# Attention into a mixture of experts on one core: every score tile in two PSUM banks of its own, one bank shared by the second attention product and the transposes of q, and a planner with other durations

## The chip, the core and the metric

The kernel runs on one core of a Trainium2 chip. The core has TensorE (PE, matrix products; its weight loads are listed as PEld), VectorE (DVE), ScalarE (ACT), GpSimd (POOL) and SyncE (SP, which here only issues DMAs). Matrix products are written to PSUM, eight banks of 2 KB in each of 128 partitions, so 512 float32 values wide; PE writes PSUM, DVE and ACT read it. The metric is the device time of one execution in microseconds, less is better. Before the change three runs took 2241.11, 2243.8 and 2248.19 us, median 2243.8.

## What is computed

```python
# attention: 4 batches of 12288 queries, 128 channels
kv_pool = kv.reshape(B, H // r, r, W // r, r, C).mean(axis=(2, 4))   # 768 keys for each batch
k = v = kv_pool.reshape(B, -1, C) @ w_sr
s = scale * (q @ k.T);  a = softmax(s);  x = a @ v                   # x: 49152 rows of 128
# mixture of experts on x: 8 experts, one for each row
logits = normalized(x) @ normalized(expert_emb).T / tau
e = argmax(logits);  gate = softmax(logits)[e]
out = gate * (relu(x @ w1[e]) @ w2[e])                               # w1: 128 x 1024, w2: 1024 x 128
```

## The kernel before

Every float32 operand of a large product is split into two float16 halves, hi and lo, and the product is made of three float16 products (hi x hi, hi x lo, lo x hi).

**Attention** runs in 96 steps of 512 queries. For each step, q is scaled, transposed and split (`q_mul`, `q_t`, `q_hi`, `q_lo`; the transposes by PE into the PSUM tile `pq`, from step 45 on by a DMA instead). Then for each of four groups of 128 queries: the score product of 128 x 768 (`s_mm`, L608, six matmuls), its negated maximum on DVE (`s_max`, L613), the scaled bias (`s_bias`, L625), the exponential on ACT (`s_exp`, L631), and the split of the result p into halves (`p_hi`, L649, and `p_lo`, L659). The halves are turned by DMA (`p_t`, L664). The second product (`av`, L679, eighteen matmuls of 137 columns for one group) writes two groups side by side into one bank, the tile `xp`; DVE inverts the sums (`x_norm`, L690 and L691), ACT or DVE scales the rows (`x_mul`, L699 or L701), and after some copies the rows are scattered to HBM by expert (`g_scatter`, POOL).

**Groups.** After every four steps a chain of small DVE and PE instructions finds each row's expert and place (`g_logits`, `g_count`, `g_rank`, `g_place`; counts in the PSUM tile `rk`), and another, on POOL and DVE in turn, chooses which tiles the experts work on (`select`, L1029 to L1081).

**Experts** take tiles of 512 rows (88 of them), then of 256 rows. A tile is loaded transposed (`load`), its expert's weights are fetched (`load_w`), and it runs in eight units: the first layer (`l1`, L1298, three matmuls of 512 columns into the tile `ph`), its two halves hh on ACT (`h_hi`, L1305) and hl on DVE (`h_lo`, L1310), and the second layer (`l2`, L1331, twelve matmuls into the tile `po`). The result is scaled (`o_out`, L1340) and scattered.

**PSUM.** In the first `ka` steps attention is alone: two score tiles of three banks, each with two scores of 768 columns side by side, so that the middle bank belongs to both (`s_tiles`, L330); and two single banks (`ps_1`, `ps_2`) in turn for everything else that goes through `one_tile`: xp, pq, rk, the products of the keys. From step `ka` on the pools are exchanged (`swap_banks`): one score tile of three banks, two banks for ph, one for po, one for xp, and one (`ps_1`) for all the rest. Instructions of two engines that touch one bank wait for each other. The step before that, `KX = KA - 1`, is the first whose xp comes from the new pool.

**The order.** The program is written in the order that a planner finds (class `Plan`). Every operation is put in by `add` with an engine, a duration in microseconds, a due time and what it waits for; the planner runs an event list over the engines, and an engine takes the ready operation that is due first. Due times come from the table `X`: lengths of a step (`da`, `di`, `db`, before, beside and after the experts) and offsets within it in eighths of a step (`av`, `l2`, `p`, `s`, `x`, `r`), or in microseconds. `turn(tag, n)` makes an operation wait for the users of the buffer n turns back, `take` and `free` hold a bank of `one_tile`. The planner lets a score wait for the score four turns back in the first stage and two turns back in the second, though the middle bank ties neighbours:

```python
tag, nb = ("s", 4) if k < KA else ("s1", 2)
o = add("PE", 0.98, key, lambda j=j: s_mm(k, j), hi, lo, *deps, *turn(tag, nb))
```

Of the kernel before, what the change touches and what calls it, by code (L numbers as in the profile page):

```python
# [33 lines left out]
P_LO = {"D": 0.87, "P": 1.6}  # L34
# [4 lines left out]
X = dict(  # L39
    ka=22, da=6.919, di=15.197, db=12.403, dma=1.46, ahead=3.016, av=9.0, av0=0.39, l2=1.971, qt=5.647,  # L40
    lead=15.443, x=4.072, r=2.598, s=-2.823, p=10.466, x0=18.227, r0=19.685, s0=2.117, p0=10.054, qt0=1.742,
    pm="cabcbcacccbccbccccacaa", pl="aaaaaaaa", nm="DD", xn="A", nm0="D", xn0="DA", we="dcdadcddaddcddcd",
    h=5.625, kv=6.596, kvs=0.535, w0=-23.865, start=21.505, early=28.723, wd=10.527, xw=0.77, qd=45, qs=4.44,
    ql=8.549, v0=47.946, m=1.536, end=-1.246, ne=-9.661, ge=-97.983,
)
# [3 lines left out]
def attention_moe(  # L49
# [280 lines left out]
    s_tiles = [ps_s.tile([P, 2 * NK], F32, name=f"s_{i}") for i in range(2)]  # L330
# [268 lines left out]
    def s_mm(k, j):  # L599
        n = NQ * k + j  # L600
        o = n % 2 * NK
        t = s_tiles[n // 2 % len(s_tiles)]
        qs, kk = ks[k]["qT"][:, j], st[k // SPB]["k"]
        cuts = (0, 256, NK) if o else (0, 512, NK)
        for lo, hi in zip(cuts, cuts[1:]):
            terms = ((0, kk[0]), (0, kk[1]), (1, kk[0]))
            for i, (l, r) in enumerate(terms):
                nc.tensor.matmul(t[:, o + lo : o + hi], qs[:, l, :], r[:, lo:hi], start=i == 0, stop=i == 2)  # L608
        ks[k]["s", j] = t[:, o : o + NK]
# [59 lines left out]
    def av(k, j):  # L669
        h, i = divmod(j, 2)  # L670
        if i == 0:
            name = f"xp{k}_{h}"
            t = one_tile(name) if k < KX else ps_h.tile([P, 512], F32, tag="xp", name=name, bufs=1)
            ks[k]["xp", h] = t[:, : 2 * VW].rearrange("p (j c) -> p j c", c=VW)
        (hi, lo), v = (ks[k]["pt", h, n][:, i] for n in range(2)), v2[k // SPB % 2]
        w = C + E + 1
        for c in range(NCH):
            for n, (l, r) in enumerate(((hi, v[0]), (hi, v[1]), (lo, v[0]))):
                nc.tensor.matmul(  # L679
                    ks[k]["xp", h][:, i, :w], l[:, c, :], r[:, c, :w], start=c == 0 and n == 0,  # L680
                    stop=c == NCH - 1 and n == 2,
                )
# [632 lines left out]
    def l2(t, u):  # L1315
        n = size(t)
        fu = 512 // n
        if u == 0:
            tag = "xp" if t >= NA and t % 2 else "po"
            ts[t]["po"] = ps_h.tile([P, n], F32, tag=tag, name=f"po{t}", bufs=1)  # L1320
# [31 lines left out]
    KX = KA - 1  # L1352
# [155 lines left out]
    def step_ops(k):  # L1508
# [3 lines left out]
        if k % 2 == 0:  # L1512
# [9 lines left out]
            qa = add("DVE", 0.65, key + 0.5, lambda: q_scale(k), *sqs, k_scale[b])  # L1522
# [19 lines left out]
        tag, nb = ("s", 4) if k < KA else ("s1", 2)  # L1542
        for j in range(NQ):
# [52 lines left out]
        for j in range(NQ):  # L1596
            h, i = divmod(j, 2)
            key = slot(k + 1, at(k, "av") + 2 * j)
            deps = [o] if j else [v_ready[b]]
            if i == 0 and k >= KX:  # L1600
                deps += [x_swap, *turn("xp", 1)]
# [4 lines left out]
            if i == 0 and k >= KX:  # L1606
                took("xp", o)
# [3 lines left out]
            if i:  # L1611
                v = add("DVE", 0.38, key + 1.2, lambda h=h: x_norm(k, h), o, *([n] if h else turn("x", 2)))
                eng = in_turn("xn", k, 2 * k + h)
                n = add(
                    eng, 0.42 if eng == "ACT" else 0.36, key + 1.5, lambda h=h: x_mul(k, h), v,
                    free=f"xp{k}_{h}" if k < KX else None,
# [4 lines left out]
                if k >= KX:  # L1621
                    reads("xp", v, n)
# [3 lines left out]
        lo = add("POOL", 1.2, key + at(k, "r"), lambda: x_lo(k), hi)  # L1626
# [5 lines left out]
    def group_ops(g, t):  # L1632
# [12 lines left out]
        for i, fn in enumerate(places):  # L1645
# [6 lines left out]
            add("POOL", 1.28, t + 1.28 * i, lambda i=i: g_scatter(g, i), pc[-1], gc[-1], dma=0.22) for i in range(GT)  # L1652
# [5 lines left out]
        if g >= 2:  # L1658
# [3 lines left out]
            for i, fn in enumerate(select(n, base[(n + 3) % 3])):  # L1662
                eng, dur = ("DVE", 0.15) if fn.__name__ in SELECT_DVE else ("POOL", 0.3)
# [40 lines left out]
    for t in range(NTILE):  # L1704
# [8 lines left out]
        lw = took("wb", add("POOL", 1.35, s - X["lead"] - 1.0, lambda t=t: load_w(t), *deps[:2], *stores, *turn("wb", WB), dma=2.92))  # L1713
        o1 = o2 = None
        f = 512 / size(t)
        for u in range(nu):
# [7 lines left out]
            po = "xp" if not whole and t % 2 else "po"  # L1724
            o2 = add("PE", 0.68, k2, lambda t=t, u=u: l2(t, u), hi, lo, o2, *(turn(po, 1) if u == 0 else ()))
# [9 lines left out]
            add("POOL", 1.28, k2 + 4.0 + 1.28 * j, lambda t=t, j=j: o_scatter(t, j), o, dma=0.2) for j in range(size(t) // P)  # L1735
# [42 lines left out]
```

## Time and profile before

| | |
|---|---|
| median of three runs | 2243.8 us (2241.11 to 2248.19) |
| the profiled execution | 2243.36 us, span 2241.7 us |
| PE busy | 1975.5 us, 88% of the span |
| DVE, ACT, POOL busy | 79%, 68%, 65% |
| score products | 53.8 to 1960.8 us |
| experts' products | 391.7 to 2230.0 us |

In the lines below, `out<-in` names the tiles without buffer numbers; "x" is a count, and a duration in a group is its mean. A line of the waits reads: engine and line that waited, engine and line that ended the wait, microseconds in total, times, the longest. In the timeline a row begins with its start and duration, and brackets give the idle time of the engine before it and what ended it. PEclk is the granted TensorE clock in tenths of full speed. The order shows what stands on an engine one after the other, with no times; line numbers there are those of the kernel it is taken from, and those of the changed kernel lie two to ten lower or higher than before.

### The profile page before, as it was taken

The numbers are of one execution on the slowest core, as the hardware profiler recorded it, in microseconds if no ns is written. First come the engines' busy times: TensorE is split into PE (matmuls) and PEld (weight loads), VectorE is DVE, ScalarE is ACT, GpSimd is POOL, SyncE is SP. The second block draws the span as 40 slices with busy tenths as digits, with TensorE's granted clock in tenths as the row PEclk, the third lists the DMA queues.
The fourth block names the chain that finished last, engine by engine and source line by source line (L and its number), as shares of the span: only waits on it lengthen the run. The fifth ranks groups of instructions, "written<-read, shape, count | busy, mean of one in ns | idle before, by whom it ended". The sixth has DMA issues, their size and how long they took to land.

```text
span 2241.7 us, 57429 instructions
## 1 busy us (share of the span) xinstructions
PE 1975.5 (88%) x21516; PEld 1492.5 (67%) x21516; DVE 1765.4 (79%) x3863; ACT 1531.3 (68%) x3158; POOL 1464.9 (65%) x1932
## 2 busy tenths in 40 slices
PE   5776765988999889898999998999999999999998
PEld 4455554766777666676766776666777766776697
DVE  6877788888878878888878878888888878865655
ACT  3677776687777667776767776777777777754443
POOL 1435268877677686686686686876686576677454
PEclk9788997999999999999999999999999999999999
DMA  8897799978778678997888897978887787743233
GB/s 233 188 209 157 156 181 197 183 149 140 158 131 151 136 137 166 167 180 137 141 158 156 137 169 143 207 146 154 134 155 145 133 160 120 134 79 81 50 86 79
DMA packets 896123, 331.86 MB, mean 148 GB/s; under 512 B 842706, under 2 KB 854107, under 8 KB 894048
## 3 DMA queue, kind: packets, MB, share of 16 engines
q1 hardware_dynamic: 853504, 258.60, 64.8%
q0 software_dynamic: 39968, 68.29, 11.0%
q8 instruction: 171, 2.80, 0.5%
q10 hardware_dynamic: 2368, 1.25, 0.2%
q14 instruction: 112, 0.92, 0.1%
HBM read 170.55 MB, written 64.50 MB: 105 GB/s over the span
## 4 chain that ended last, share of the span: by engine, by line
DVE 27%; PE 27%; POOL 17%; ACT 13%; issue 12%; DMA 4%; POOLq 0%; SPq 0%; DVEq 0%; ACTq 0%
POOL xs_rows L183 8%; PE po L1331 7%; PE s L608 7%; PE ph L1298 7%; DVE plo L659 7%; DVE nm L613 6%; ACT p L631 6%; PE xp L679 5%; DVE hl L1310 5%; POOL out_dram L183 3%; ACT phi L649 2%; ACT hh L1305 2%; POOL t_part L1023 2%; ACT x L699 1%; DVE nm L625 1%
## 5 line engine op out<-in xcount | busy, mean ns | idle before, releaser
L1305 ACT ACTIVATE hh<-ph 128x512 f16<-128x512 f32 x776 | 463.2, 597 | 340.4 <-PE ph L1298 286.0
L1310 DVE SCALAR_TENSOR_TENSOR hl<-ph,hh 128x512 f16<-128x512 f32 x776 | 530.0, 685 | 141.1 <-ACT hh L1305 135.9
L1298 PE MATMUL ph<-x,wbuf 128*128 128x512 f16 (+1 forms) x2544 | 623.5, 362 | 1.8 <-DVE hl L1310 1.3
L1331 PE MATMUL po<-wbuf,hh 128*128 128x128 f16 x6208 | 610.9, 219 | 8.3 <-DVE o L1340 8.2
L1331 PE MATMUL po<-wbuf,hl 128*128 128x128 f16 x3104 | 560.2, 220 | 36.1 <-DVE hl L1310 34.4
L608 PE MATMUL s<-k,qT 128*128 128x512 f16 (+1 forms) x2304 | 454.0, 336 | 134.4 <-ACT p L631 98.4
L1331 PEld LDWEIGHTS <-hh 128*128 128x128 f16 x6208 | 498.5, 98 | 80.1 <-issue 13.2
L631 ACT ACTIVATE p<-s,nm,qa 128x768 f32<-128x768 f32 x384 | 380.2, 991 | 249.1 <-DVE nm L625 136.6
L183 POOL DMA_INDIRECT out_dram<-o,m x388 | 415.7, 1071 | 183.5 <-issue 101.0
L183 POOL DMA_INDIRECT xs_rows<-rows,pi x384 | 421.6, 1098 | 120.0 <-issue 101.6
L679 PE MATMUL xp<-v,pthi 128*128 128x137 f16 x4608 | 467.5, 227 | 24.1 <-DVE x L701 18.0
L659 DVE TENSOR_TENSOR plo<-p,phi 128x768 f16<-128x768 f32 x371 | 402.8, 1087 | 69.3 <-ACT phi L649 64.2
L679 PEld LDWEIGHTS <-pthi 128*128 128x128 f16 x4608 | 385.2, 100 | 100.5 <-issue 32.5
L608 PEld LDWEIGHTS <-qT 128*128 128x128 f16 x2304 | 228.2, 100 | 326.8 <-issue 177.8
L679 PE MATMUL xp<-v,ptlo 128*128 128x137 f16 x2304 | 444.4, 226 | 0.6 <-DMA ptlo<-plo 0.6
L613 DVE TENSOR_REDUCE nm<-s 128x1 f32<-128x768 f32 x384 | 364.9, 950 | 75.9 <-PE s L608 40.9
L1331 PEld LDWEIGHTS <-hl 128*128 128x128 f16 x3104 | 304.0, 98 | 54.8 <-DVE hl L1310 52.9
L649 ACT CAST phi<-p 128x768 f16<-128x768 f32 x380 | 315.4, 832 | 4.3
L1298 PEld LDWEIGHTS <-wbuf 128*128 128x128 f16 x2544 | 219.9, 98 | 101.6 <-issue 6.3
L679 PEld LDWEIGHTS <-ptlo 128*128 128x128 f16 x2304 | 227.1, 99 | 0.8 <-DMA ptlo<-plo 0.8
L723 POOL COPY x<-x 128x32 f32<-128x32 f32 x96 | 33.2, 345 | 198.5 <-ACT x L699 198.3
L1258 POOL DMA_INDIRECT wbuf<-w_prep,wi_i x106 | 117.0, 1104 | 56.6 <-issue 19.7
(338 smaller groups left out, 1911.7 us busy)
## 6 DMA issues: line engine op xcount, KB each, us to landing
q<-in_q_dram SPq DMA_DIRECT2D x96, 256.0 KB
kvt<-in_kv_dram SPq DMA_DIRECT2D x64, 384.0 KB
wf<-in_moe_w_dram SPq DMA_DIRECT2D x16, 512.0 KB
out_dram<-o,m POOLq DMA_INDIRECT x388
xs_rows<-rows,pi POOLq DMA_INDIRECT x384
w_prep<-wo SPq DMA_DIRECT2D x8, 514.0 KB
w_prep<-wo SPq DMA_DIRECT2D x8, 512.0 KB
x<-xs_rows SPq DMA_TRANSPOSE x212
```

Of the source, the lines that this page charges most:

```text
L183: ins = nc.gpsimd.indirect_dma_start(out=dst[:, :], out_offset=bass.IndirectOffsetOnAxis(ap=idx, axis=0), in_=src, in_offset=None, bounds_ ...
L608: nc.tensor.matmul(t[:, o + lo : o + hi], qs[:, l, :], r[:, lo:hi], start=i == 0, stop=i == 2)
L613: V.tensor_reduce(out=nm, in_=ks[k]["s", j], axis=AX.X, op=ALU.max, negate=True)
L631: nc.scalar.activation(out=p, in_=ks[k].pop(("s", j)), func=AF.Exp, bias=ks[k].pop(("nm", j)), scale=ks[k]["fac"],)
L649: nc.scalar.copy(out=hi, in_=p)
L659: eng.tensor_tensor(out=lo, in0=ks[k].pop(("p", j)), in1=hi, op=ALU.subtract)
L679: nc.tensor.matmul(ks[k]["xp", h][:, i, :w], l[:, c, :], r[:, c, :w], start=c == 0 and n == 0, stop=c == NCH - 1 and n == 2,)
L1258: nc.gpsimd.indirect_dma_start(out=wbuf[t % WB][:, :], out_offset=None, in_=wprep[:, :], in_offset=bass.IndirectOffsetOnAxis(ap=wi_i[:, t ...
L1298: nc.tensor.matmul(ph[:, kk * n : (kk + 1) * n], wt[:, o + f : o + f + P], r, start=i == 0, stop=i == 2)
L1305: nc.scalar.activation(out=hh, in_=ts[t]["ph", u], func=AF.Relu)
L1310: V.scalar_tensor_tensor(out=hl, in0=ts[t].pop(("ph", u)), scalar=0.0, in1=ts[t]["hh", u], op0=ALU.max, op1=ALU.subtract)
L1331: nc.tensor.matmul(po[:, j * C : (j + 1) * C], l[:, js], wt[:, o : o + P], start=first, stop=last, skip_group_check=True,)
```

## The change

Every score gets a PSUM tile of two banks: three such tiles in the first stage, two in the second. To make room in the second stage (4 + 2 + 1 + 1 banks), xp loses its own bank and takes turns with pq, rk and the key products in `ps_1` at every step. The odd ones of the last tiles of 256 rows take their po from the pool that follows the scores. In the planner, a score waits for the score three turns back in the first stage; the two halves of a second product are due by `4 * h + avd * i` eighths instead of `2 * j`; many durations are other numbers. In the table, `ka` goes from 22 to 24 (attention alone for two more steps), `qd` from 45 to 41 (q is turned by DMA from step 41), and the offsets are other numbers.

```diff
-P_LO = {"D": 0.87, "P": 1.6}
+P_LO = {"D": 0.94, "P": 1.6}
+SELECT_TWO = ("left", "skip", "passed", "wrap", "begin", "lead_rows", "row")
...
-    ka=22, da=6.919, di=15.197, db=12.403, dma=1.46, ahead=3.016, av=9.0, av0=0.39, l2=1.971, qt=5.647,
+    ka=24, da=6.919, di=11.199, db=8.301, dma=1.6, ahead=3.046, av=10.77, av0=0.881, l2=1.792, qt=5.916,
...
-    s_tiles = [ps_s.tile([P, 2 * NK], F32, name=f"s_{i}") for i in range(2)]
+    s_tiles = [ps_s.tile([P, 2, 512], F32, name=f"s_{i}").rearrange("p a b -> p (a b)") for i in range(3)]
...
     def s_mm(k, j):
-        n = NQ * k + j
-        o = n % 2 * NK
-        t = s_tiles[n // 2 % len(s_tiles)]
+        t = s_tiles[(NQ * (k - KA) + j) % len(s_tiles)]
         qs, kk = ks[k]["qT"][:, j], st[k // SPB]["k"]
-        cuts = (0, 256, NK) if o else (0, 512, NK)
-        for lo, hi in zip(cuts, cuts[1:]):
+        for lo, hi in ((0, 512), (512, NK)):
             terms = ((0, kk[0]), (0, kk[1]), (1, kk[0]))
             for i, (l, r) in enumerate(terms):
-                nc.tensor.matmul(t[:, o + lo : o + hi], qs[:, l, :], r[:, lo:hi], start=i == 0, stop=i == 2)
-        ks[k]["s", j] = t[:, o : o + NK]
+                nc.tensor.matmul(t[:, lo:hi], qs[:, l, :], r[:, lo:hi], start=i == 0, stop=i == 2)
+        ks[k]["s", j] = t[:, :NK]
...
     def av(k, j):
         h, i = divmod(j, 2)
         if i == 0:
-            name = f"xp{k}_{h}"
-            t = one_tile(name) if k < KX else ps_h.tile([P, 512], F32, tag="xp", name=name, bufs=1)
-            ks[k]["xp", h] = t[:, : 2 * VW].rearrange("p (j c) -> p j c", c=VW)
+            ks[k]["xp", h] = one_tile(f"xp{k}_{h}")[:, : 2 * VW].rearrange("p (j c) -> p j c", c=VW)
...
-            tag = "xp" if t >= NA and t % 2 else "po"
-            ts[t]["po"] = ps_h.tile([P, n], F32, tag=tag, name=f"po{t}", bufs=1)
+            pool = ps_s if t >= NA and t % 2 else ps_h
+            ts[t]["po"] = pool.tile([P, n], F32, tag="po", name=f"po{t}", bufs=1)
...
-        tag, nb = ("s", 4) if k < KA else ("s1", 2)
+        tag, nb = ("s", 3) if k < KA else ("s1", 2)
...
-            o = add("PE", 0.98, key, lambda j=j: s_mm(k, j), hi, lo, *deps, *turn(tag, nb))
+            o = add("PE", 1.0, key, lambda j=j: s_mm(k, j), hi, lo, *deps, *turn(tag, nb))
...
-            key = slot(k + 1, at(k, "av") + 2 * j)
+            key = slot(k + 1, at(k, "av") + 4 * h + X["avd"] * i)
...
-                "PE", 1.05, key, lambda j=j: av(k, j), rowed[k, h, 0], rowed[k, h, 1], *deps,
-                take=f"xp{k}_{h}" if i == 0 and k < KX else None,
-            )
+                "PE", 1.08, key, lambda j=j: av(k, j), rowed[k, h, 0], rowed[k, h, 1], *deps,
+                take=f"xp{k}_{h}" if i == 0 else None,
+            )
...
-                eng, dur = ("DVE", 0.15) if fn.__name__ in SELECT_DVE else ("POOL", 0.3)
+                eng, dur = ("DVE", 0.2) if fn.__name__ in SELECT_DVE else ("POOL", 0.75 if fn.__name__ in SELECT_TWO else 0.42)
...
-            s_tiles[:] = [ps_s.tile([P, 2 * NK], F32, name="s_2")]
+            s_tiles[:] = [
+                ps_s.tile([P, 2, 512], F32, name=f"s1_{i}").rearrange("p a b -> p (a b)") for i in range(2)
+            ]
```

More of the change, by code (lines that the diff above doesn't have):

```diff
@@ L1351, in attention_moe @@
     KA = X["ka"]
-    KX = KA - 1
     TS = [0.0]
@@ L1521, in step_ops @@
                 loads.append(ql)
-            qa = add("DVE", 0.65, key + 0.5, lambda: q_scale(k), *sqs, k_scale[b])
+            qa = add("DVE", 1.0, key + 0.5, lambda: q_scale(k), *sqs, k_scale[b])
             reads("qa", qa)
@@ L1547, in step_ops @@
                 deps = deps + k_ready[b]
-            o = add("PE", 0.98, key, lambda j=j: s_mm(k, j), hi, lo, *deps, *turn(tag, nb))
+            o = add("PE", 1.0, key, lambda j=j: s_mm(k, j), hi, lo, *deps, *turn(tag, nb))
             took(tag, o)
             reads("qT", o)
-            m = took("nm", add("DVE", 0.98, key + at(k, "s"), lambda j=j: s_max(k, j), o, *turn("nm", 4)))
+            m = took("nm", add("DVE", 0.87, key + at(k, "s"), lambda j=j: s_max(k, j), o, *turn("nm", 4)))
             eng = in_turn("nm", k, NQ * k + j)
-            z = add(eng, 0.2 if eng == "ACT" else 0.13, key + at(k, "s") + 0.5, lambda j=j: s_bias(k, j), m)
+            z = add(eng, 0.29 if eng == "ACT" else 0.13, key + at(k, "s") + 0.5, lambda j=j: s_bias(k, j), m)
             e = add("ACT", 0.89, key + at(k, "s") + 1.0, lambda j=j: s_exp(k, j), z, *turn("p", 4))
@@ L1588, in step_ops @@
             x_swap = add(
-                "-", 0.0, TS[k + 1], lambda: swap_banks(False), *[o for u in uses["s"][-4:] for o in u],
+                "-", 0.0, TS[k + 1], lambda: swap_banks(False), *[o for u in uses["s"][-3:] for o in u],
                 take="give up",
@@ L1611, in step_ops @@
             if i:
-                v = add("DVE", 0.38, key + 1.2, lambda h=h: x_norm(k, h), o, *([n] if h else turn("x", 2)))
+                v = add("DVE", 0.33, key + 1.2, lambda h=h: x_norm(k, h), o, *([n] if h else turn("x", 2)))
                 eng = in_turn("xn", k, 2 * k + h)
                 n = add(
-                    eng, 0.42 if eng == "ACT" else 0.36, key + 1.5, lambda h=h: x_mul(k, h), v,
-                    free=f"xp{k}_{h}" if k < KX else None,
+                    eng, 0.54 if eng == "ACT" else 0.36, key + 1.5, lambda h=h: x_mul(k, h), v,
+                    free=f"xp{k}_{h}",
                 )
@@ L1620, in step_ops @@
                     took("x", v)
-                if k >= KX:
-                    reads("xp", v, n)
         av_last[b] = [o]
@@ L1625, in step_ops @@
         lg = add("POOL", 0.25, key + at(k, "x"), lambda: x_lg(k), *ns, chained[g])
-        lo = add("POOL", 1.2, key + at(k, "r"), lambda: x_lo(k), hi)
+        lo = add("POOL", 1.28, key + at(k, "r"), lambda: x_lo(k), hi)
         sq = [add("ACT", 0.3, key + at(k, "r") + 1.0 + 0.3 * j, lambda j=j: x_sq(k, j), ns[j // 2], chained[g]) for j in range(NQ)]
@@ L1651, in group_ops @@
         sc = [
-            add("POOL", 1.28, t + 1.28 * i, lambda i=i: g_scatter(g, i), pc[-1], gc[-1], dma=0.22) for i in range(GT)
+            add("POOL", 1.37, t + 1.37 * i, lambda i=i: g_scatter(g, i), pc[-1], gc[-1], dma=0.22) for i in range(GT)
         ]
@@ L1712, in attention_moe @@
         took("m", ld)
-        lw = took("wb", add("POOL", 1.35, s - X["lead"] - 1.0, lambda t=t: load_w(t), *deps[:2], *stores, *turn("wb", WB), dma=2.92))
+        lw = took("wb", add("POOL", 1.4, s - X["lead"] - 1.0, lambda t=t: load_w(t), *deps[:2], *stores, *turn("wb", WB), dma=2.92))
         o1 = o2 = None
@@ L1723, in attention_moe @@
             reads(tag, hi, lo)
-            po = "xp" if not whole and t % 2 else "po"
-            o2 = add("PE", 0.68, k2, lambda t=t, u=u: l2(t, u), hi, lo, o2, *(turn(po, 1) if u == 0 else ()))
+            po = "po2" if not whole and t % 2 else "po"
+            o2 = add(
+                "PE", 0.72, k2, lambda t=t, u=u: l2(t, u), hi, lo, o2,
+                *((*turn(po, 1), x_last if po == "po2" else None) if u == 0 else ()),
+            )
             if u == 0:
@@ L1734, in attention_moe @@
         sc = [
-            add("POOL", 1.28, k2 + 4.0 + 1.28 * j, lambda t=t, j=j: o_scatter(t, j), o, dma=0.2) for j in range(size(t) // P)
+            add("POOL", 1.34, k2 + 4.0 + 1.34 * j, lambda t=t, j=j: o_scatter(t, j), o, dma=0.2) for j in range(size(t) // P)
         ]
```

12 lines of the change are left out of this document (4 added, 8 removed).

## The prediction

> **What bounds the kernel now.** I read the page first, then busy time by stage, then what TensorE (PE) waits for in the longest stage, then one step of the timeline.
>
> From the page, the span, busy times, the granted clock and the DMA share in 40 slices:
>
> ```profile
> span 2241.7 us, 57429 instructions
> PE 1975.5 (88%) x21516; PEld 1492.5 (67%) x21516; DVE 1765.4 (79%) x3863; ACT 1531.3 (68%) x3158; POOL 1464.9 (65%) x1932
> PEclk9788997999999999999999999999999999999999
> DMA  8897799978778678997888897978887787743233
> ```
>
> The first and last score product (L608) and first-layer product (L1298) set the stages; the rows give them by line.
>
> ```profile
> L608 PE MATMUL s<-k,qT x2304: 269/376/634, 53.8 to 1960.8; 128*128 128x512 f16 x192
> L1298 PE MATMUL ph<-x,wbuf x2544: 272/379/634, 391.7 to 2230.0; 128*128 128x512 f16 x163, 128*128 128x256 f16 x33
> ```
>
> Stage A (0 to 392) is attention alone, 22 steps; stage B (392 to 1960) runs the other 74 steps beside experts' tiles; stage C (to 2241.7) is experts alone. Busy time by stretch (PE, PEld, DVE, ACT, POOL, then clock, DMA share, GB/s), a piece of A first:
>
> ```profile
> 280.00:360.00 80.00, 55.28 (x561) 42.66 (x560) 68.84 (x154) 58.78 (x120) 54.93 (x70) 0.96 0.95 176
> 392.00:1960.00 1568.00, 1448.09 (x16150) 1087.66 (x16149) 1295.85 (x2873) 1147.10 (x2419) 1112.94 (x1511) 1.00 0.82 151
> 1960.00:2241.00 281.00, 268.79 (x3220) 213.15 (x3217) 161.20 (x306) 122.30 (x225) 175.41 (x213) 0.99 0.33 76
> ```
>
> B and C are PE's: it is busy for 92% and 96%. The end of A is not: PE is at 69%, DVE at 86%, the DMA engines at 0.95. B has 1568 - 1448 = 120 us of idle PE, and this is what ends it:
>
> ```profile
> PE s L608 <- ACT p L631: 55.4, 67, 2.9
> PE po L1331 <- DVE hl L1310: 32.3, 42, 3.2
> PE s L608 <- DVE nm L613: 10.9, 10, 3.9
> PE po L1331 <- DVE o L1340: 8.2, 13, 1.3
> ```
>
> A score product waits for the exponential (L631) or the maximum (L613) of another score: 66.3 us, 77 times, never longer than 3.9. In B one tile of three banks holds two scores and the middle bank belongs to both, so the next score cannot be written before the last one has been read out. The two readers pay as well: in B the maximum waits for the other score's exponential (ACT), and the exponential for the other score's product (the two lines that follow, each with its busy time, mean, and idle time by releaser).
>
> ```profile
> L631 ACT ACTIVATE p<-s,nm,qa 128x768 f32<-128x768 f32 x294 | 291.5, 991 | 185.9 <-DVE nm L625 136.6 <-PE s L608 35.7 <-DVE nm L613 3.9
> L613 DVE TENSOR_REDUCE nm<-s 128x1 f32<-128x768 f32 x295 | 280.2, 950 | 32.4 <-ACT p L631 17.3 <-PE s L608 13.0 <-ACT phi L649 1.0
> L625 DVE TENSOR_SCALAR nm<-nm,qa 128x1 f32<-128x1 f32 x294 | 60.4, 205 | 1.8
> ```
>
> **PE's own work in a step of B**, from starts of the timeline:
>
> ```profile
> 1002.34 0.81 PE L1298 MATMUL ph<-x,wbuf 128*128 128x512 f16 x3
> ...
> 1002.98 0.28 PE L679 MATMUL xp<-v,pthi 128*128 128x137 f16 x2
> ...
> 1003.18 0.60 ACT L1305 ACTIVATE hh<-ph 128x512 f16<-128x512 f32 x1 [1.18 <-PE ph L1298]
> ...
> 1003.28 0.68 DVE L1310 SCALAR_TENSOR_TENSOR hl<-ph,hh 128x512 f16<-128x512 f32 x1
> ...
> 1004.07 0.28 PE L1331 MATMUL po<-wbuf,hh 128*128 128x128 f16 x2
> ...
> 1004.74 0.81 PE L1298 MATMUL ph<-x,wbuf 128*128 128x512 f16 x3
> ...
> 1005.39 1.14 PE L608 MATMUL s<-k,qT 128*128 128x512 f16 x6
> ...
> 1006.37 0.28 PE L1331 MATMUL po<-wbuf,hh 128*128 128x128 f16 x2
> ```
>
> A first-layer unit takes 1002.98 - 1002.34 = 0.64 us, a second attention product 1.09, a second-layer unit 0.67, a score 0.98. A step with a tile is 4 x (0.98 + 1.09) + 8 x (0.64 + 0.67) = 18.8 us; it takes 1568 / 74 = 21.2.
>
> **The change, part by part.** *Two banks for every score.* After its product a score needs 0.95 + 0.21 + 0.99 us (the three lines above) and some four hand-overs of up to 0.20 (1002.98 to 1003.18, PE to ACT): about 2.7 us. Counted over PE's whole order with the durations just read, the next score starts 3.5 to 4 us after a score's end in 171 of 295 places of B, mostly 3.7 to 3.8, which leaves 1 us for whatever else is queued on DVE and ACT. After the change a score waits only for the one before the last. The engine here is ACT, in step 58, before; p is a score's exponential, hh a unit's first half, s_2 the one shared tile:
>
> ```order
> L631 ACTIVATE p58_0_19780<-s_2_4659,nm58_0_19728,qa58_18108 128x768
> L1305 ACTIVATE hh36_1_19796<-ph36_1_19782 128x512
> L649 CAST phi58_0_19805<-p58_0_19780 128x768
> L1305 ACTIVATE hh36_2_19851<-ph36_2_19828 128x512
> L631 ACTIVATE p58_1_19862<-s_2_4659,nm58_1_19823,qa58_18108 128x768
> L649 CAST phi58_0_19805<-p58_1_19862 128x768
> L699 ACTIVATE x56_19887<-xp56_0_19732,rn56_0_19888 128x136 x2
> ```
>
> And the same place of ACT's order after it:
>
> ```order
> L629 ACTIVATE p58_0_19364<-s1_0_5266,nm58_0_19325,qa58_17724 128x768
> L1301 ACTIVATE hh34_1_19380<-ph34_1_19366 128x512
> L647 CAST phi58_0_19387<-p58_0_19364 128x768
> L574 ACTIVATE q2_61_19445<-q61_19015,qa60_18480 128x4x128
> L629 ACTIVATE p58_1_19457<-s1_1_5267,nm58_1_19410,qa58_17724 128x768
> L1301 ACTIVATE hh34_2_19479<-ph34_2_19448 128x512
> L647 CAST phi58_0_19387<-p58_1_19457 128x768
> ```
>
> The scores of the step now alternate between s1_0 and s1_1, and tile 34 instead of 36 stands beside it. By PE's order the score before the last is 8.4 us back at the median (3.6 in the three closest places): 4.6 us more than 3.8, while no wait was longer than 3.9. So nearly all 66.3 us go: 66.3 x 72 / 74 = 64.5, of which I leave 2. What comes late next is the pair hh, hl that a second-layer unit waits for.
>
> *That pair.* A unit's halves need 0.20 + 0.60 + 0.68 us (rows above) and two hand-overs, some 1.7 us. Counted over PE's orders for the first 72 tiles, the second layer follows the first of the same unit by less than 3 us of PE's work in 52 of 576 units before and in 220 after, where it is mostly 2.3 instead of 3.4. Now 32.3 us / 74 tiles / 8 = 0.055 us are waited per unit. Nothing more is one end; one wait of the mean length 32.3 / 42 = 0.77 in each of 168 more units, 129 us, is the other. I take one more 0.055 for each, +10 us, since a margin of 0.6 us over 1.7 still covers most single neighbours on ACT and DVE.
>
> *One bank for the second product, the transposes and the counts.* Before, xp had a bank of its own in B. Its place in PE's order before:
>
> ```order
> L679 LDWEIGHTS ptlo25_1_6748
> L679 MATMUL xp25_1_7047<-v0_1_108,ptlo25_1_6748 128x137
> L341 MATMUL pq28_7077<-ident_58,q28_6533 128x128 x4
> L608 LDWEIGHTS qT27_6772
> L608 MATMUL s_2_4659<-k0_1_5552,qT27_6772 128x256
> ```
>
> After, the transposes pq28 of step 28 stand between units:
>
> ```order
> L1327 LDWEIGHTS hl3_3_6706
> L1327 MATMUL po3_6598<-wbuf0_2395,hl3_3_6706 128x128
> L342 MATMUL pq28_6734<-ident_58,q28_5618 128x128 x4
> L1294 LDWEIGHTS wbuf0_2395
> L1294 MATMUL ph3_5_6743<-x_3_5630,wbuf0_2395 128x512
> ```
>
> They have moved off the end of a product, with 2.3 us of other PE work or more before the next user of the bank in most places. To free it, a transpose needs ACT, then DVE, and a product two ACT instructions:
>
> ```profile
> L576 ACT CAST qT<-pq 128x512 f16<-128x512 f32 x22 | 12.8, 582 | 0.7 <-PE pq L341 0.7
> L587 DVE TENSOR_TENSOR qT<-pq,qT 128x512 f16<-128x512 f32 x22 | 15.1, 687 | 5.0 <-ACT qT L576 5.0
> L699 ACT ACTIVATE x<-xp,rn 128x136 f32<-128x136 f32 x292 | 92.9, 371 | 21.6 <-DVE rn L691 19.7 <-DVE n6z L751 1.3 <-issue 0.4
> ```
>
> That is 0.58 + 0.69 + 0.4 of hand-overs = 1.7 us. By the order of after, 50 hand-overs of the bank in B have under 2.5 us of PE work in between. The ends are 0 and 50 x 0.77 = 39 us; I take +6, nearer to the low one, because it is the same 1.7 against 2.3 as for the pair. Where PE does wait there, the next unit's first layer is queued behind it, and ACT's hh and DVE's hl wait for that.
>
> *The order by new durations.* The choice of tiles ties DVE to POOL; first and last of six such rows of B (together 88.6 us of DVE's idle time):
>
> ```profile
> DVE t_lt L1127 <- POOL t_cum L1119: 21.9, 18, 1.6
> ...
> DVE t_st L1105 <- POOL t_pas L1024: 8.0, 9, 1.8
> ```
>
> The planner's numbers for those POOL steps rise (0.3 to 0.42 or 0.75), and by DVE's order more of DVE's other work stands between two of them (from the running sum L1049 to the reduction L1105, the lower quartile goes from 2.0 to 4.0 us at the rows' durations). DVE's lateness reaches PE only as the wait for hl. Ends 0 and -16, half of that wait; I take -8. The four steps that now turn q by DMA (41 to 44) put four more transfers on SP's queue, ahead of turns of p there, and take four steps' transposes and their copies off PE and ACT: four steps of 72 with one copy of 0.58 us less each (L576 above) against one transfer more: I set them at nothing.
>
> *Two more steps in A, two tiles moved to C.* Of A's pace the row is
>
> ```profile
> 280.00:360.00 80.00, 25.40 (x138) 13.04 (x137) 0.96 0.95 176
> ```
>
> (L608 alone): 138 / 24 = 5.75 steps in 80 us, 13.9 each; two more are +28. Own banks help A too, but DMA at 0.95 leaves little: ends 0 and -30, I take -5. In C two whole tiles come to 2 x 8 x 1.31 = +21.
>
> **The sum.** A 392 + 28 - 5 = 415; B 72 x 21.2 = 1526, less 62.5, less 8, plus 10, plus 6 = 1471 (20.4 a step); C 281 + 21 = 302. That is 2188; the profiled execution took 2243.4 with its span of 2241.7, so 2190. It was 0.4 below the median, which is in the rounding: **2190 us**, 2.4% less.
>
> **The rivals.** (1) *The waits only move.* DVE is busy for 83% of B and the pace stays 21.2: A 420, B 1526, C 302, and 2: 2250, no change. For it: 66.3 us of PE's waits also let DVE and ACT catch up. Against it: DVE has 17% left, and 17.3 and 35.7 us of the readers' own waits (above) go as well. (2) *PE runs close to its own pace*, 19.6 a step: 415 + 1411 + 302 + 2 = 2130. For it: in C, where nothing but the pair is waited for, PE is at 96%. (3) *Slower: the pair hh, hl.* If the 168 tighter units wait 0.55 us each on average, 92 us instead of 10, the end is 2190 + 82 = 2272; it decides from (2244 + 7 - 2190 + 10) / 168 = 0.42 us on. Against it: the units wait in 42 of 592 cases now. (4) *Slower: the one bank.* If every one of the 196 hand-overs that the order shows in B left 0.5 us open, 98 us instead of 6, it is 2282. Against it: most have over 4 us of PE work in between. The Trainium skill speaks for (4): its page "Perfetto Trace Analysis", section Matmuls, has independent groups go round through different PSUM banks so that one's evacuation lies under the next one's matmuls, and this change gives that up for xp, pq and the counts while restoring it for the scores. By that rule the change loses on this bank; the trace agrees with it for the scores (66.3 us), and no run here shows it for xp and pq in one bank.
>
> **How the numbers follow.** The forecast (2155 to 2225, most of the way to the ends of its small terms) has 0.55, (2) 0.20, a halved gain between 2225 and 2237 0.06; (1) has 0.07, (3) 0.08, (4) 0.04. About 0.3%, 7 us, is what a measurement of this kernel can tell from no change. So faster 0.81, same 0.07, slower 0.12. The range leaves out the far ends of (2), (3) and (4): 2130 to 2245.
>
> **What would show it.** Right: in the new profile the rows "PE s <- ACT p" and "PE s <- DVE nm" of B nearly vanish, a step takes near 20.4 us, the first expert's matmul stands near 415, the last score near 1886. Wrong: "PE po <- DVE hl" far above 45 us (3), a row "PE xp <- DVE qT" or "PE pq <- ACT x" above 20 us (4), or DVE at 90% of B at an unchanged pace (1).

## The result, and the profile after

The changed kernel takes 2174.28 us (median of four runs, 2167.3 to 2177.87) where the kernel before takes 2243.8 beside it: a ratio of 0.9685, 95% interval 0.9655 to 0.9714, 69.5 us less. The forecast was 2190, range 2130 to 2245. Its profiled execution took 2172.59 us.

The page after, with the span, busy times and DMA shares by slice:

```profile
span 2170.9 us, 57378 instructions
PE 1959.6 (90%) x21500; PEld 1484.5 (68%) x21500; DVE 1781.7 (82%) x3868; ACT 1508.2 (69%) x3147; POOL 1473.5 (68%) x1932
DMA  8899999988769779897889889988779778532243
```

First and last start of the score products (L606 now) and of the experts' first layer (L1294), which bound the stages:

```profile
L606 PE MATMUL s<-k,qT x2304: 272/376/634, 53.3 to 1868.7; 128*128 128x512 f16 x192
L1294 PE MATMUL ph<-x,wbuf x2544: 272/379/634, 400.6 to 2157.3; 128*128 128x512 f16 x163, 128*128 128x256 f16 x33
```

So A ends at 400.6 (forecast 415), B takes 1868.7 - 400.6 = 1468.1 us, 20.39 for each of its 72 steps (forecast 1471 and 20.4), and C 2170.9 - 1868.7 = 302.2 (forecast 302). Busy times by stretch, a piece of A first, then B and C:

```profile
280.00:360.00 80.00, 46.34 (x385) 32.32 (x385) 68.94 (x143) 53.90 (x114) 61.51 (x80) 0.78 0.95 195
400.00:1868.00 1468.00, 1397.36 (x15628) 1052.04 (x15626) 1268.00 (x2787) 1096.38 (x2351) 1072.68 (x1450) 0.99 0.84 156
1868.00:2170.00 302.00, 290.00 (x3460) 228.59 (x3457) 172.71 (x323) 131.06 (x241) 187.24 (x227) 0.99 0.33 74
```

PE is idle for 71 us of B instead of 120 (117 for 72 of the 74 steps), and busy for 95% instead of 92%. The step is 0.8 us shorter, 58 us in 72 steps; 46 of them are idle time that is gone, and why PE's busy time is some 12 us less for the same steps is not shown. What ends its idle time in B now:

```profile
PE po L1327 <- DVE o L1336: 18.5, 21, 3.2
PE po L1327 <- DVE hl L1306: 17.7, 36, 1.9
PE rk L821 <- DVE oh L807: 7.8, 8, 2.3
PE xp L675 <- DVE qT L588: 4.7, 3, 3.7
...
PE s L606 <- ACT p L629: 0.6, 1, 0.6
```

The scores wait 0.6 us where they waited 66.3. The wait for hl fell from 32.3 to 17.7, the wait for o (a finished tile's scaling, which empties the bank po) rose from 8.2 to 18.5. The scores' two readers in B no longer wait for the neighbour:

```profile
L629 ACT ACTIVATE p<-s,nm,qa 128x768 f32<-128x768 f32 x287 | 284.7, 992 | 208.3 <-DVE nm L623 151.4 <-PE ph L1294 15.5 <-DVE y L778 7.0
L611 DVE TENSOR_REDUCE nm<-s 128x1 f32<-128x768 f32 x287 | 271.4, 946 | 1.2 <-PE s L606 1.1
```

The maximum had 32 us of idle time ahead of it before and has 1.2 now; its wait for ACT's exponential is gone. DVE's waits for POOL in the choice of tiles have fallen from 90 us to 25 (all their rows together; here the longest row and one of the smaller ones):

```profile
DVE t_lt L1123 <- POOL t_cum L1115: 6.2, 6, 2.6
...
DVE t_st L1101 <- POOL t_pas L1020: 3.4, 6, 0.9
```

### The profile page after: what moved, and what is told of

It is laid out like the page before. It is cut to its first block, busy times and chain, and to the rows that moved or that the text cites. A ratio compares the mean times of both kernels' runs of the same rounds, so it can differ in the third digit from the quotient of the medians.

```text
span 2170.9 us, 57378 instructions
## 1 busy us (share of the span) xinstructions
PE 1959.6 (90%) x21500; PEld 1484.5 (68%) x21500; DVE 1781.7 (82%) x3868; ACT 1508.2 (69%) x3147; POOL 1473.5 (68%) x1932
## 4 chain that ended last, share of the span: by engine, by line
DVE 28%; PE 28%; ACT 13%; POOL 11%; issue 9%; DMA 2%; SPq 0%; POOLq 0%; DVEq 0%; ACTq 0%
PE po L1327 10%; PE ph L1294 9%; DVE nm L611 6%; DVE hl L1306 6%; DVE plo L657 5%; PE xp L675 5%; POOL xs_rows L184 4%; ACT p L629 4%; PE s L606 4%; ACT hh L1301 3%; POOL out_dram L184 2%; ACT phi L647 2%; ACT x L695 2%; DVE o L1336 1%; DVE nm L623 1%
## 5 line engine op out<-in xcount | busy, mean ns | idle before, releaser
L1294 PE MATMUL ph<-x,wbuf 128*128 128x512 f16 (+1 forms) x2544 | 625.2, 362 | 3.7 <-DVE hl L1306 3.4
L184 POOL DMA_INDIRECT xs_rows<-rows,pi x384 | 415.9, 1083 | 135.5 <-issue 108.0
L606 PE MATMUL s<-k,qT 128*128 128x512 f16 (+1 forms) x2304 | 449.4, 334 | 61.4 <-ACT p L629 59.3
L606 PEld LDWEIGHTS <-qT 128*128 128x128 f16 x2304 | 227.8, 99 | 288.0 <-issue 82.4
L675 PEld LDWEIGHTS <-pthi 128*128 128x128 f16 x4608 | 380.0, 100 | 63.0 <-issue 17.4
L657 DVE TENSOR_TENSOR plo<-p,phi 128x768 f16<-128x768 f32 x371 | 383.6, 1037 | 22.7 <-ACT phi L647 18.9
L611 DVE TENSOR_REDUCE nm<-s 128x1 f32<-128x768 f32 x384 | 363.4, 946 | 18.8 <-PE s L606 15.4
L1294 PEld LDWEIGHTS <-wbuf 128*128 128x128 f16 x2544 | 219.9, 98 | 99.9 <-issue 10.0
L695 ACT ACTIVATE x<-xp,rn 128x136 f32<-128x136 f32 x336 | 107.5, 373 | 69.6 <-DVE rn L687 47.2
```

The costliest lines, as they stand in the source:

```text
L184: ins = nc.gpsimd.indirect_dma_start(out=dst[:, :], out_offset=bass.IndirectOffsetOnAxis(ap=idx, axis=0), in_=src, in_offset=None, bounds_ ...
L606: nc.tensor.matmul(t[:, lo:hi], qs[:, l, :], r[:, lo:hi], start=i == 0, stop=i == 2)
L611: V.tensor_reduce(out=nm, in_=ks[k]["s", j], axis=AX.X, op=ALU.max, negate=True)
L657: eng.tensor_tensor(out=lo, in0=ks[k].pop(("p", j)), in1=hi, op=ALU.subtract)
L675: nc.tensor.matmul(ks[k]["xp", h][:, i, :w], l[:, c, :], r[:, c, :w], start=c == 0 and n == 0, stop=c == NCH - 1 and n == 2,)
L695: nc.scalar.mul(x[:, i, :], xp[:, i, : C + E], rn[:, i, :])
```

## The experiments

The theory is that of the prediction: in B, PE waited for the scores' shared bank, and taking that away carries the gain, with the order by new durations as a small help. The main rival is that the waits only move, and the order (or something else in the new numbers) carries the gain.

Four kernels (shared_late, select_old, banks_alone, numbers_alone) ran first on a chip that was slower with every kernel: the kernel before took 2522.88 us there, and in the traces from there the engines also stand still for nothing that the profile shows. All four were run again on another chip, and their readings below are from there; `_b` marks them. That chip was used for two sets of runs, in which the kernel before took 2242.75 and 2242.3 us: the first held the changed kernel, shared_late_b, shared_early and o_first, the second the others. So three of the `_b` kernels and qd24 are held against the changed kernel across two sets, whose kernels before differ by 0.45 us. In the tables, A ends with the first expert's product, B with the last score, and C with the span; "scores", "hl", "o" are PE's waits in B for the readers of scores, for hl and for o, the next column is the sum of all rows of PE's waits in B, and "choice" is DVE's waits for POOL in the choice of tiles, all in us.

| kernel | median | ratio to before, 95% | A | B, and for each step | C |
|---|---|---|---|---|---|
| before | 2242.75 | 1 | 391.7 | 1569.1, 21.20 | 280.9 |
| after_again | 2173.83 | 0.9701 (0.968 to 0.9722) | 401.6 | 1468.1, 20.39 | 301.3 |
| shared_late_b | 2211.09 | 0.9869 (0.9848 to 0.989) | 403.6 | 1508.2, 20.95 | 299.4 |
| select_old_b | 2218.05 | 0.9895 (0.9879 to 0.9912) | 405.6 | 1508.6, 20.95 | 302.1 |
| banks_alone_b | 2206.03 | 0.9832 (0.9816 to 0.9848) | 366.6 | 1555.1, 21.02 | 282.5 |
| numbers_alone_b | 2262.33 | 1.0092 (1.0078 to 1.0106) | 448.2 | 1511.3, 20.99 | 300.8 |
| shared_early | 2176.59 | 0.9717 (0.9696 to 0.9737) | 404.1 | 1469.0, 20.40 | 301.7 |
| o_first | 2177.02 | 0.9709 (0.9688 to 0.973) | 403.7 | 1474.0, 20.47 | 302.9 |
| qd24 | 2188.27 | 0.976 (0.9743 to 0.9776) | 411.8 | 1470.3, 20.42 | 301.6 |

(The stages of the kernel before are those of its profile above; it and banks_alone_b have 74 steps in B, the others 72.)

| in B | scores | hl | o | all of PE's waits | choice |
|---|---|---|---|---|---|
| before | 66.3 | 32.3 | 8.2 | 118 | 90 |
| after_again | 0.6 | 17.9 | 18.2 | 71 | 23 |
| shared_late_b | 60.0 | 10.6 | 4.9 | 100 | 15 |
| select_old_b | 0.2 | 47.2 | 23.5 | 100 | 85 |
| banks_alone_b | 1.5 | 63.0 | 11.7 | 105 | 96 |
| numbers_alone_b | 58.1 | 13.1 | 6.9 | 109 | 9 |

**The changed kernel again (after_again).** No edit.

> The changed kernel again, beside the kernel before and the three kernels below on one chip, so that each can be held against it. By the first measurement of it the ratio to the kernel before is 0.97 (0.9655 to 0.9714), on a chip where the kernel before took 2244 us. On a slower chip, where every engine also stands still for nothing that the profile shows, the absolute savings should be kept and the ratio with them: 0.965 to 0.975. If the savings depended on how closely the engines follow each other, the ratio would move towards 0.98 there.

It took 2173.83 us, 0.9701 of the kernel before: the first result holds, and the kernels below are held against it. It did not run on the slower chip, so how the ratio fares there stays open.

**Scores of B tied again (shared_late, shared_late_b).** The two scores of a pair stand side by side in three banks again, in B only; the order of every engine stays that of the changed kernel.

```diff
-        t = s_tiles[(NQ * (k - KA) + j) % len(s_tiles)]
+        n = NQ * (k - KA) + j
+        o = n % 2 * NK if k >= KA else 0
+        t = s_tiles[0 if k >= KA else n % len(s_tiles)]
...
-            s_tiles[:] = [
-                ps_s.tile([P, 2, 512], F32, name=f"s1_{i}").rearrange("p a b -> p (a b)") for i in range(2)
-            ]
+            s_tiles[:] = [ps_s.tile([P, 2 * NK], F32, name="s_2")]
```

> The changed kernel with one thing undone: in stage B the two scores stand again side by side in one tile of three banks, sharing the middle one; every engine's order stays as it is. Theory 1 (a score's own banks bring the gain of B): PE's waits for L629 and L611 before a score, under 1 us in B of the changed kernel, come back to about 60 us, and the time goes up by 50 to 90 us, to 2225 to 2265. Theory 2 (the new order brings it, the banks hardly matter): under 10 us more, 2175 to 2185. Theory 3 (both needed): the order puts some scores closer behind each other than the old one did (2.6 us of PE's work in a quarter of the places, where a score needs 2.7), so it is slower than the kernel before, 2265 or more.

> The changed kernel with the two scores of stage B side by side in three banks again, all orders unchanged, this time beside the changed kernel on one chip. Theory 1 (the tie of two scores through the middle bank is what PE waited for): the waits of PE's scores for the exponential come back with 55 to 70 us in B, and the time is 45 to 65 us above the changed kernel (ratio to before 0.99 to 1.0). Theory 2 (the order was what mattered, waits only move): the waits come back but displace others, and the time is at most 20 us above it.

PE's waits in B in shared_late_b (its L609, L632, L614 are the score product, exponential and maximum):

```profile
PE s L609 <- ACT p L632: 53.1, 95, 3.1
PE po L1330 <- DVE hl L1309: 10.6, 23, 1.4
PE rk L824 <- DVE oh L810: 7.5, 9, 1.9
PE s L609 <- DVE nm L614: 6.9, 7, 2.3
PE po L1330 <- DVE o L1339: 4.9, 10, 0.8
```

The 60 us of score waits are back, as theory 1 has it, but the time rises by 37.3 us (B by 40.1), between the two theories' figures for shared_late_b. The waits for hl and o fall from 36.1 to 15.5, which fits DVE catching up while PE waits for a score. A wait of the scores is worth some 0.6 of its length here. On the slower chip (ratio to before 0.9805, 0.9736 to 0.9873) nothing can be said, since the changed kernel did not run there.

**Old durations for the choice of tiles (select_old, select_old_b).**

```diff
-                eng, dur = ("DVE", 0.2) if fn.__name__ in SELECT_DVE else ("POOL", 0.75 if fn.__name__ in SELECT_TWO else 0.42)
+                eng, dur = ("DVE", 0.15) if fn.__name__ in SELECT_DVE else ("POOL", 0.3)
```

> The changed kernel with the planner's old durations for the choice of tiles alone (0.15 on DVE and 0.3 on POOL instead of 0.2 and 0.42 or 0.75). The prediction's term was 8 us for them: 2178 to 2190. A rival, after the trace of the changed kernel, in which DVE's six waits for POOL fell from 89 to about 23 us in B while PE's wait for hl fell from 32 to 18: these numbers are worth 25 to 45 us, 2200 to 2220, with those waits back above 70 us.

> The changed kernel with the two old durations for the choice of tiles (0.15 us on DVE, 0.3 on POOL), so that the planner again puts DVE's steps of the choice close behind POOL's. Theory 1 (the prediction's term: DVE stands waiting for POOL, and PE's wait for hl follows): DVE's waits in the choice rise from 23 to over 60 us, the wait for hl by 5 to 15, the time by 5 to 15 us. Theory 2 (DVE's lateness there is covered): DVE's waits rise, the time stays within 5 us.

PE's waits in B of select_old_b, and three of DVE's for POOL:

```profile
PE po L1327 <- DVE hl L1306: 47.2, 56, 2.9
PE po L1327 <- DVE o L1336: 23.5, 23, 5.0
PE ph L1294 <- DVE hl L1306: 9.0, 6, 3.4
```

```profile
DVE t_lt L1123 <- POOL t_cum L1115: 20.4, 16, 4.1
DVE t_ex L1164 <- POOL t_ex L1159: 18.1, 12, 4.1
...
DVE t_first L1148 <- POOL t_hit L1145: 17.1, 14, 2.7
```

These durations in the planner cost 44.2 us, three times the upper end of what theory 1 gave for select_old_b (on the slower chip the ratio to before was 0.9833, 0.9771 to 0.9895). The direction is theory 1's: DVE stands for POOL again (23 to 85 us), and the waits for hl, o and the next ph rise from 40.7 to 79.7. This is as large as undoing the banks. In all runs of the table DVE's waits go with these durations: 85 to 96 us with the old ones, 9 to 23 with the new ones. The other offsets were left as they are for the new durations, and whether others would have made up for the old ones is not shown; with the whole old table a step of B is as long (21.02 us in banks_alone_b, the next experiment).

**The banks alone (banks_alone, banks_alone_b).** The changed kernel with the table and the durations of before (ka = 22, di = 15.197 and so on, and avd = 2.0, the old distance of the halves), so the planner orders by the old numbers.

```diff
-    ka=24, da=6.919, di=11.199, db=8.301, dma=1.6, ahead=3.046, av=10.77, av0=0.881, l2=1.792, qt=5.916,
+    ka=22, da=6.919, di=15.197, db=12.403, dma=1.46, ahead=3.016, av=9.0, av0=0.39, l2=1.971, qt=5.647,
...
-                eng, dur = ("DVE", 0.2) if fn.__name__ in SELECT_DVE else ("POOL", 0.75 if fn.__name__ in SELECT_TWO else 0.42)
+                eng, dur = ("DVE", 0.15) if fn.__name__ in SELECT_DVE else ("POOL", 0.3)
```

> The changed kernel's banks (two for each score, one shared by xp, the transposes and the counts) with the table and all durations of the kernel before: 22 steps in stage A, the planner's old offsets. Theory 1: most of the gain stays, stage B at 20.3 to 20.7 us a step for 74 steps, 2180 to 2205 in all. Theory 2: 2230 to 2250, because the waits move to the shared bank and to DVE. The waits of DVE for POOL in the choice of tiles stay near 89 us in both.

> The changed banks alone: every score in two banks and xp in the shared bank, with the table and the durations of before, so the planner writes an order by the old numbers (22 steps in stage A). Theory 1 (the banks carry the gain, the order the rest): PE's waits for the exponential are gone from B, and the time is 35 to 50 us under the kernel before, ratio 0.978 to 0.985. Theory 2 (the waits only move without an order made for it): the waits for hl, o and the shared bank take over 50 us of the 66, and the ratio is over 0.992.

The ratio, 0.983 on both chips, is the one that theory 1 named, but the stages show it for another reason. PE's and DVE's waits in B of banks_alone_b:

```profile
PE po L1327 <- DVE hl L1306: 63.0, 75, 2.8
PE po L1327 <- DVE o L1336: 11.7, 9, 3.0
```

```profile
DVE t_first L1148 <- POOL t_hit L1145: 22.9, 18, 2.3
DVE et L1134 <- POOL t_lt L1131: 20.7, 16, 2.6
```

In B only 14.0 of 1569.1 us are gained, though 65 us of score waits are gone: the wait for hl has doubled, from 32.3 to 63.0, and DVE still stands 96 us for POOL. By its waits theory 2 is right for B, though its ratio is not: hl and o take 34 of the 65 us, smaller rows another 17, and all of PE's waits together fall by 13. In B the rival that the waits only move is what happened. The rest of the gain is stage A, 25.1 us shorter.

**The numbers alone (numbers_alone, numbers_alone_b).** The kernel before, its banks kept, with the new table and durations and the new due times of the second product's halves.

```diff
-            key = slot(k + 1, at(k, "av") + 2 * j)
+            key = slot(k + 1, at(k, "av") + 4 * h + X["avd"] * i)
...
-                eng, dur = ("DVE", 0.15) if fn.__name__ in SELECT_DVE else ("POOL", 0.3)
+                eng, dur = ("DVE", 0.2) if fn.__name__ in SELECT_DVE else ("POOL", 0.75 if fn.__name__ in SELECT_TWO else 0.42)
```

> The kernel before with the changed table and durations, and its own banks (two scores share the middle one, xp has a bank). Theory 1: no faster than before, 2235 to 2260, since the score waits stay and two more steps of attention alone cost about 7 us net. Theory 2: 2175 to 2195. The waits of DVE for POOL in the choice of tiles fall below 35 us in both.

> The new table and durations alone, with the banks of before: the two scores of B in three banks, xp in a bank of its own. The kernel with only B's scores tied again stood 37 us above the changed kernel and 32 us under the one before; this one differs from it by xp's own bank and stage A's pairs. Theory 1 (one bank for xp, pq and the counts costs a few us, stage A's pairs 3): the time is 2200 to 2215 us, ratio 0.981 to 0.988. Theory 2 (these numbers are worth nothing without the other banks, as one run on a slower chip had it with 1.0035): ratio 0.995 to 1.005, with stage A 15 us or more later.

PE's waits in B of numbers_alone_b:

```profile
PE s L609 <- ACT p L632: 53.7, 96, 2.8
PE po L1332 <- DVE hl L1311: 13.1, 16, 3.3
...
PE po L1332 <- DVE o L1341: 6.9, 11, 1.0
```

It is slower than the kernel before, by 20 us (1.0035 on the slower chip): theory 2, and outside its range of ratios. DVE's waits for POOL are nearly gone (9 us) and hl is cheap, but the scores still wait 58 us. Its B of 1511.3 us is close to that of shared_late_b (1508.2), which has xp in the shared bank: an own bank for xp brings no gain that can be seen there, though the two differ in their order as well, which the planner wrote for other banks. (The expectation took xp's bank and the pairs of A for the only differences.) Its A is 46.6 us longer than that of the changed kernel. In the order of the changed kernel pairs of scores are not the reason, by the next experiment. What is left is the order that the planner writes under the old rules (a score waits four turns back). From the first score on, a step of A takes 15.4 and 16.5 us under that rule (before, numbers_alone_b), and 14.2, 14.4 and 14.6 us with three turns (banks_alone_b, after_again, shared_early), under either table and with either layout of the banks.

**Scores of A tied again (shared_early).** Only in the first 24 steps, with the order of the changed kernel.

```diff
-        t = s_tiles[(NQ * (k - KA) + j) % len(s_tiles)]
+        n = NQ * k + j
+        o = n % 2 * NK if k < KA else 0
+        t = s_tiles[n // 2 % 2 if k < KA else n % 2]
```

> The changed kernel with only the scores of stage A (the first 24 steps) in pairs in three banks again, stage B as changed. It asks where stage A's unforeseen 14 us came from. Theory 1 (the own banks of A's scores): the first expert's matmul comes 15 to 25 us later, near 415 to 420 where the changed kernel has 400.6, and the waits of A's scores rise by as much. Theory 2 (the order by new durations, with A held by DVE and the DMA engines): it comes within 5 us of the changed kernel's, the time unchanged.

A ends at 404.1 against 401.6, the time is 2.8 us more, the runs overlap (2175.5 to 2181.07 against 2171.29 to 2178.35), and kernels with the very same A end it between 400.6 and 403.6 (after, after_again, shared_late_b). Theory 2: with this order the scores' own banks are worth nothing in A that can be told from the spread. The waits of A's scores, of shared_early and then of after_again:

```profile
PE s L609 <- ACT p L632: 37.6, 23, 7.8
PE s L609 <- DVE nm L614: 19.6, 13, 3.9
```

```profile
PE s L606 <- ACT p L629: 57.0, 44, 5.0
```

57.2 and 57.0: the sum is the same; it is only the other reader that ends them.

**o first on DVE (o_first).**

```diff
-        o = took("o", add("DVE", 0.66 / f, k2 + 0.8, lambda t=t: o_out(t), o2, *turn("o", 2)))
+        o = took("o", add("DVE", 0.66 / f, k2 - 4.0, lambda t=t: o_out(t), o2, *turn("o", 2)))
```

> The changed kernel with one due time changed: the scaling of a finished tile on DVE (o from po) is due 4.8 us earlier, so that DVE takes it first as soon as the tile's last product is done. It asks whether PE's wait for it, which rose from 8.2 to 18.5 us in B, is a cost of the change that can be had back. Theory 1 (DVE does other work first, and PE's next tile waits): the wait falls below 8 us and the time by 5 to 12 us, 0.2 to 0.5%. Theory 2 (PE's waits move to the hl that DVE now does later): the wait falls, the wait for hl rises from 17.7 by as much, and the time stays within 5 us.

It took 2177.02 us, 3.2 more, with runs that overlap (2173.23 to 2182.37). PE's waits in B (the profiled execution is the slowest, 2182.37):

```profile
PE po L1327 <- DVE hl L1306: 25.6, 36, 3.9
PE po L1327 <- DVE o L1336: 20.1, 19, 3.9
```

The time is that of theory 2, the waits are those of neither: the wait for o did not even fall, and the one for hl rose by 7.7. What makes o late is shown further down by one place of the changed kernel.

**q turned by DMA from step 24 (qd24).**

```diff
-    h=6.389, kv=7.574, kvs=0.535, w0=-23.865, start=22.304, early=28.723, wd=10.527, xw=1.009, qd=41, qs=5.17,
+    h=6.389, kv=7.574, kvs=0.535, w0=-23.865, start=22.304, early=28.723, wd=10.527, xw=1.009, qd=24, qs=5.17,
```

> The changed kernel with q turned by DMA from step 24 on, where the changed kernel does so from 41: in B the bank that xp, pq and the counts share has no pq any more, and PE, ACT and DVE lose 17 steps' transposes and copies, for 17 more transfers on SP's queue. Theory 1 (the shared bank costs what the prediction took, 6 us, and pq a third of it): the waits of PE for the copies of pq (4.7 us) vanish and the time is 0 to 8 us less. Theory 2 (the bank costs more than its waits show, since the planner keeps it free for pq): 10 to 20 us less. Theory 3 (transfers are what is short in that stretch): the loads of the tiles come later and the time rises by 5 us or more.

It is 14.4 us slower, the way that theory 3 has it, and 10.2 of them are in A. PE's waits at the end of A and the beginning of B, from 340 to 412:

```profile
PE xp L675 <- DVE x L697: 12.3, 1, 12.3
PE xp L675 <- DMA pthi<-phi: 7.4, 1, 7.4
...
PE xp L675 <- DMA ptlo<-plo: 3.2, 1, 3.2
```

The first of them is in after_again too; the two waits for a turned p, 10.6 us, are not there (none of its rows for these tiles reaches 0.5 us). Seventeen more steps' turns of q go through SP's queue, as those of p do, and the DMA engines are 0.95 busy in the stretch of A shown above; that the turns of q delay those of p is not shown beyond this. What PE waits for there is the turned p, not the tiles' loads that theory 3 named. The wait xp <- qT (4.7 us) goes as it should, but the wait for hl in B is 30.3 us instead of 17.9, and B, 1470.3 against 1468.1, gains nothing: what a bank without pq is worth by itself stays open.

None of these kernels beats the changed one.

## Why the prediction was right, and where its terms were not

**The sum was right, two of its terms were not, and that they made up for each other is luck.** B was forecast at 1471 and took 1468.1, C at 302 and took 302.2. But "less 62.5" for the score waits and "less 8" for the order do not hold by themselves: undone alone, the first costs 40.1 us of B and the second 40.5 (shared_late_b, select_old_b), together more than the 58 us by which B shrank (72 x 21.20 = 1526 to 1468). The two help each other. By the pace of B: the old banks and numbers 21.20, the banks alone 21.02, the numbers alone 20.99, both 20.39. Each alone brings 0.2 us a step, both bring 0.8. Taken one after the other, the banks bring 13 us in 72 steps (72 x 0.18, forecast 62.5) and the numbers on top of them 45 (72 x 0.63, forecast 8): the mechanism that the prediction named for the gain does not carry it without the term that it held for small.

**The step that failed** is "DVE's lateness reaches PE only as the wait for hl. Ends 0 and -16, half of that wait; I take -8." That bound was read from a trace with 66 us of score waits, beside which a late DVE showed as 32.3 us of waits for hl. With the score waits gone it is more: 63.0 us for hl in banks_alone_b, and 39 us of waits for hl, o and ph in select_old_b over those of the changed kernel. One such place in the changed kernel: PE after a score, then the waiting second layer.

```profile
1011.89 1.14 PE L606 MATMUL s<-k,qT 128*128 128x512 f16 x6
1016.04 0.27 PE L1327 MATMUL po<-wbuf,hh 128*128 128x128 f16 x2 [3.02 <-DVE o L1336]
```

And DVE there:

```profile
1015.02 0.17 DVE L1164 SCALAR_TENSOR_TENSOR t_ex<-t_ex,t_nt 128x8 f32<-128x8 f32 x1 [2.52 <-POOL t_ex L1159]
1015.24 0.75 DVE L1336 SCALAR_TENSOR_TENSOR o<-po,wbuf,m 128x512 f32<-128x512 f32 x1
```

And POOL:

```profile
1013.73 0.99 POOL L184 DMA_INDIRECT out_dram<-o,m  x1 [1.97 <-issue]
1014.78 0.20 POOL L1159 TENSOR_SCALAR t_ex<-t_ex 128x8 f32<-128x8 f32 x1
```

DVE stands 2.52 us for one small step of POOL, with o queued behind it, and PE stands for o. The wait of PE names o; what was late is t_ex. POOL's step itself takes 0.20 us, but it stands behind the scatter of an earlier tile's rows, 0.99 us after 1.97 us in which POOL waited for nothing that the profile shows. So the step came later than its own length, or the planner's 0.42 us for it, would have it. An earlier due time for o did not shorten the waits for o (20.1 us in o_first, 18.2 without).

**The score waits.** That they would go was right to within 2 us (66.3 to 0.6, where 2 were forecast to stay). That a wait of 62.5 us is worth 62.5 was not: put back, it is worth 40.1. The prediction did name what comes late next, the pair, but priced it by its own tighter distance alone.

**The pair hh, hl.** Forecast was +10 for its tighter place and -8 for the order, so 32.3 x 72 / 74 + 2 = 33 us of wait for hl; it was 17.7. So the units did not pay for the tighter place as far as the row shows, and rival (3) with 92 us is out. No run changed the pair's distance by itself.

**The one bank** was forecast at +6. Its rows in B are xp <- qT with 4.7 and smaller ones, some 9 us; B is no shorter with an own bank for xp (numbers_alone_b, 3 us above shared_late_b) nor without pq in the bank (qd24). Neither run takes the bank alone (other orders, tied scores, or a longer wait for hl), so its price by itself is not shown; rival (4) with 98 us is out, since B took 1468.1. By the rule of the Trainium skill that the prediction weighed ("Perfetto Trace Analysis", section Matmuls, groups go round through different banks), the change should have lost on this bank. The traces agree with the rule for the scores in B, where a tie costs 37 us. For the scores in A a tie costs 2.8 us, which is within the spread, and for xp, pq and counts no run shows a loss or takes the bank alone. That other work of PE between two users of a bank decides it is argued, not shown.

**Stage A** was forecast at 415 and took 400.6: the term "-5" was -19. Not by the banks (shared_early: 2.5). banks_alone_b, whose scores the planner spaces by the new rule, three turns back instead of four, ends its 22 steps at 366.6 instead of 391.7, with the old table. So the order carries it, which the prediction had looked at in B only. The kernels of the experiments that are ordered by three turns have steps of 14.2 to 14.9 us there from the first score on, and the two ordered by four turns have 15.4 and 16.5; no run changes that rule alone, so that it is the rule is likely and not shown.

**The rivals.** (1), the waits only move, is what the banks alone do in B (14 us of 65); it fails for the whole because with the new durations the next wait in line does not come (47.2 us for hl in select_old_b, 17.9 without). (2), 19.6 us a step, was too far: 71 us of idle PE stay.

## What to carry to other kernels

Before a removed wait is counted in full, look for the engine that the wait let catch up: here 60 us of PE's waits were worth 37, and with the old order 65 us of them were worth 14 in that stage, where the waits for hl rose from 32 to 63. Such limits are priced by undoing one at a time in the new kernel as well as by doing one at a time in the old one; the two disagree where they help each other. And two durations in a planner's table (POOL's steps at 0.3 us or at 0.42 and 0.75, DVE's at 0.15 or 0.2) were worth as much in the changed kernel as a new layout of the banks.

## What the runs showed of the hardware

**A long wait has an echo.** After the 3.02 us above PE's clock falls: slices of a microsecond from the same place (the last three columns are the granted clock, the DMA share and GB/s).

```profile
1016.00:1017.00 1.00, 0.96 (x17) 0.95 (x17) 1.00 (x2) 0.00 (x0) 0.80 (x3) 0.94 0.74 282
1017.00:1018.00 1.00, 1.00 (x11) 1.00 (x10) 1.00 (x2) 0.00 (x0) 0.97 (x2) 0.50 0.02 5
...
1020.00:1021.00 1.00, 1.00 (x17) 1.00 (x16) 0.00 (x0) 0.87 (x2) 0.47 (x2) 0.85 0.20 74
1021.00:1022.00 1.00, 1.00 (x19) 0.95 (x17) 0.59 (x3) 0.60 (x2) 1.00 (x2) 1.00 0.00 0
```

By these shares the clock is halved from about 1016.9 to 1020.3; at full clock the work of those 3.4 us takes 1.7, so another 1.7 us came on top of the 3.02. In B of this trace the clock falls five times, each time for some 3.4 us, and each time after one of the five waits of PE of 2.95 us and more (2.95 to 3.69); after the next longest, 2.27 us, it does not. In B of the kernel before it falls four times, after waits of 2.21, 2.47, 3.20 and 3.92 us, and not after two of 2.31 and 2.90. So in these traces the length alone does not decide it. The Trainium skill's page "TensorE: Matmul & The Clock Gate", in Part 1, has the clock fall to half after an idle window of some 3.4 us; here shorter waits, from 2.21 us on, were followed by it.

**One chip was 12.5% slower** with the same kernel (2522.88 us against 2242.3). The kernel of select_old, traced on both, has waits that the profile puts down to nothing of 92.9 us on PE, 134.4 on DVE and 32.8 on ACT there, and of 0.5, 0.9 and 2.6 us on the other chip (select_old_b). What holds the engines there is not shown. Ratios to the kernel before differ by at most 0.7% between the two chips (there and here: 0.983 and 0.9832 for the banks alone, 0.9805 and 0.9869 for the tied scores, 1.0035 and 1.0092 for the numbers alone, 0.9833 and 0.9895 for the old durations).
